# Sums of squares of two chunks, moved on ScalarE from the first feed-forward stage into the opening stage of a delta-rule kernel

## The chip, the core and the metric

The kernel runs on one core of one Trainium2 chip. Five engines of the core work side by side, each through its own list of instructions, strictly in order: TensorE (PE, matrix products and transposes, with its weight loads shown apart as PEld), VectorE (DVE), ScalarE (ACT), GpSimd (POOL) and SyncE (SP, which here only issues transfers). An engine whose next instruction waits for another engine does nothing until that wait is over, even if later instructions of its list could run. The metric is the time of one execution on the device in microseconds (us). Seven runs of the kernel before have a median of 671.46 us, from 670.96 to 672.62.

## What is computed

The first half is a delta-rule attention over 768 tokens, 4 batches and 8 heads of width 48. Keys are divided by their norm, and each head keeps a 48x48 state:

```python
k_n = k / (np.linalg.norm(k, axis=-1, keepdims=True) + 1e-06)
for t in range(S):
    kt, vt, bt = (k_n[:, :, t], v[:, :, t], beta[:, :, t, None])
    y[:, :, t] = np.einsum('bhd,bhde->bhe', q[:, :, t], state)
    v_old = np.einsum('bhde,bhd->bhe', state, kt)
    state = state + bt[:, :, :, None] * np.einsum('bhd,bhe->bhde', kt, vt - v_old)
```

The second half is a feed-forward layer over the 3072 token rows of width 384: `h = x @ w_in` (2048 columns), exact Gelu, and `@ w_out` back to 384 columns. The weights arrive as 64-bit floats.

## The kernel before

Tokens are cut into twelve chunks of 64. A unit is one chunk of two batches, so a chunk has two units (`u.a` is 0 or 1), and a unit's keys are a tile of 128 partitions (2 batches x 64 tokens) by 8 heads by 48. Chunks are worked in pairs, called groups: group 0 is chunks 0 and 1, group 1 is chunks 2 and 3. Within a chunk the recurrence becomes a triangular system. Its diagonal 32x32 blocks are inverted on VectorE by 30 row steps (`eliminate`, L442 and L444, two instructions each), the blocks are joined by small matmuls (`join`, L484, L495, L499), and the result, `Zf`, is multiplied with the right-hand sides (`solve`, L597, copied from PSUM by ScalarE at L603). Then come the outputs (`use`, `read`, L615, L636), their transposes (`turn`, L659, L660), the state update (L624, L629) and the feed-forward layer of the chunk (`fc1` L677 with its Gelu L679 on ScalarE, `fc2` L690).

The kernel has two parts.

The first part, from `load_v(0)` at L827 to L911, is the opening stage. In it the order on all five engines is the order in which the instructions stand in the program (`manual_schedule` over all of them). It loads the keys and queries of chunks 0 and 1, squares and sums their keys, makes their Gram products, starts the row steps of group 0 on VectorE, and while these run lets TensorE and ScalarE make the transposed queries of chunks 0 and 1 (`transposed(u, (1,))`), the score products (`queries`) and the transposes and Gram products of chunks 2 (`third`) and 3 (`fourth`). Each of these is a step of TensorE into PSUM followed by a copy on ScalarE: `Qt` and `Kt` at L347, `P` at L399, `G` at L378, `diag` at L382 and L385. PSUM results of the transposes share two buffers (tag `sq`), products share two others (tag `dn`), so TensorE can be at most two results ahead of ScalarE's copies. The keys of chunk 3 lie in `Qp[2]` and `Qp[3]` in this stage and are loaded again into `Kp` later. After the row steps come the joins, `Zf` (L457 on VectorE, the zeroing L464 and copies L499 on ScalarE), the solve of chunk 0, its outputs, and the decoding of the first pieces of the 64-bit weights. Decoding piece n takes four VectorE steps and one of ScalarE: `begin` (L218), `exponents` (L223, on ScalarE), `mantissas` (L228, L230), `signed` (L235, L236); `signed` needs the result of `exponents`. After `signed`, SyncE fetches another raw piece into the space just freed (L210).

The second part is a plan: every step has a due time in units of chunks (`at(first, last, steps)`), and all steps are written out in the order of their due times (L810). On VectorE that written order is kept. On the other engines a planner orders the instructions by that sequence and by when its own cost model believes their inputs to be ready. The decode of pieces 3 to 15 is in the plan between 0.985 and 1.65. The 32 sums of squares for chunks 2 and 3, `sum_of_squares(u, h)`, one per unit and head, are due between 1.08 and 1.5: an ACTIVATE with the function Square on 128x48 elements at L291, with the sum over the 48 taken from ScalarE's accumulator, which shows in the profile as a second instruction, ACTIVATION_READ_ACCUMULATOR. Their results lie in one tile, `ns["both"]`; its square root is taken on GpSimd at 1.51 (`prep`, L306), and the factors of group 1 are made from it on VectorE at 1.65 (`finish_both`, L265 to L269).

Of the kernel before, what the change touches and what calls it, by code (L numbers as in the profile page):

```python
# [8 lines left out]
F32 = mybir.dt.float32  # L9
# [3 lines left out]
ACT = mybir.ActivationFunctionType  # L13
# [3 lines left out]
def kernel(  # L17
# [28 lines left out]
    nc = tc.nc  # L46
    B, H, S, D = q.shape
# [5 lines left out]
    NA = B // 2  # L53
# [9 lines left out]
    wk = ctx.enter_context(tc.tile_pool(name="wk", bufs=2))  # L63
# [8 lines left out]
    def sq(name, *shape):  # L72
        return small[0].tile([128, *shape], F32, tag="sq", name=name)
# [4 lines left out]
    Qp = [cpool.tile([128, H, C], F32, name=f"Qp{i}") for i in range(NQS)]  # L78
# [12 lines left out]
    tiles = {}  # L91
# [7 lines left out]
    for c in range(NC):  # L99
        for a in range(NA):  # L100
            u = tiles[c, a] = Unit()
# [37 lines left out]
    def load_v(c):  # L139
        if c >= NC:  # L140
            return
        for a in range(NA):
            u = tiles[c, a]
            u.V = io.tile([128, H, D], F32, tag="V", name="V", bufs=4)
            fetch_in(u.V, v, u)
# [111 lines left out]
    def heads(ap):  # L257
        return ap.rearrange("q (j r) d -> q r j d", r=2)
# [24 lines left out]
    def sum_of_squares(u, h):  # L283

        if "both" not in ns:
            n23 = wk.tile([128, 2 * NA, H], F32, tag="n0", name="n0", bufs=1)
            ns[2], ns[3] = n23[:, 0:NA], n23[:, NA:]
            ns["both"] = n23
        if h == 0:
            u.ksq = wk.tile([128, H, D], F32, tag="ksq", name="ksq")  # L290
        nc.scalar.activation(u.ksq[:, h], u.Kn[:, h, 0:D], ACT.Square,  # L291
                             accum_out=ns[u.c][:, u.a, h:h + 1])

    def prep(c):
# [40 lines left out]
    def transposed(u, part=(0, 1)):  # L335
        for x in part:
            if x == 0:
                dst = u.Kt = wk.tile([128, 2, NP, C], F32, tag="Kt", name="Kt", bufs=6)
            elif u.c == 1:
                dst = u.Qt = su.tile([128, 2, NP, C], F32, tag="Qt1", name="Qt1")  # L340
            else:
                dst = u.Qt = wk.tile([128, 2, NP, C], F32, tag="Qt", name="Qt")
            psT = sq("psT", NP, 128)
            flat = (Qp[2 + u.a] if u.c == 3 and x == 0 else (u.Kp, u.Qp)[x]).rearrange("q h d -> q (h d)")
            for j in range(NP):
                nc.tensor.transpose(psT[:, j, :], flat[:, j * 128:(j + 1) * 128], ident)  # L346
            nc.scalar.copy(dst.rearrange("q p j n -> q j p n"),  # L347
                           psT.rearrange("q j (p n) -> q j p n", p=2))
# [11 lines left out]
    def products(us, x):  # L360

        psG = dn("psG").rearrange("q r (m n) -> q r m n", n=C)
        for i, u in enumerate(us):
            for j in range(NP):
                for r, p in QUADS:
                    rows = slice(r * C, r * C + D)
                    nc.tensor.matmul(psG[HALF[p], r, i * NP + j, :], lhsT=u.Kt[rows, p, j, :],  # L367
                                     rhs=(u.Qt if x else u.Kt)[rows, p, j, :],
                                     start=True, stop=True)
        return psG[:, :, 0:len(us) * NP]  # L370

    def grams(us):
        g = us[0].c // 2
        psG = products(us, 0)
        if us[0].t == 0:
            Gs[g] = (wk if g else su).tile([128, NU, HB], F32, tag="G", name="G", bufs=1)
        span = slice(us[0].t * H, (us[-1].t + 1) * H)
        nc.scalar.copy(heads(Gs[g][:, span]), psG[:, :, :, HB:C])  # L378
        if g > 0:
            if us[0].t == 0:  # L380
                Ds[g] = wk.tile([128, NU, HB], F32, tag="diag", name="diag", bufs=1)
            nc.scalar.copy(heads(Ds[g][:, span]), psG[:, :, :, 0:HB])  # L382
            for p in range(2):
                lower = slice(p * C + HB, (p + 1) * C)
                nc.scalar.copy(Ds[g][lower, span], Gs[g][lower, span])  # L385
# [3 lines left out]
    def queries(us):  # L389
        c = us[0].c  # L390
        psP = products(us, 1)
        if c not in Ps:
            Ps[c] = (su if c == 1 else wk).tile([128, NA * H, C], F32, tag=f"P{c == 1}", name="P",
                                                bufs=1)
        for u in us:
            u.P = Ps[c][:, u.a * H:(u.a + 1) * H]
        dst = heads(Ps[c][:, us[0].a * H:(us[-1].a + 1) * H])
        if c < 2:
            nc.scalar.copy(dst, psP)  # L399
        else:  # L400
            both = mask.unsqueeze(1).to_broadcast([128, len(us) * H, C])
            nc.vector.tensor_tensor(dst, psP, heads(both), op=ALU.mult)  # L402
# [259 lines left out]
    def state_steps(c):  # L662
        us = [tiles[c, a] for a in range(NA)]
        steps = [(3.0, against_state, us), (2.0, solve, us), (3.0, outputs, us)]
        return steps + [(0.5, turn, u) for u in us]
# [126 lines left out]
    def ffn_steps(c):  # L792
        ones = [(1.3, fc1, c, f) for f in range(NF)]
        if c > 1:
            return [(1.3, first_layer, c, f) for f in range(NF)] + [
                (2.6, second_layer, c, n) for n in (1, 5, 2, 6, 4, 7, 3)]
        twos = [(2.7, fc2, tiles[c, a], f, f + 4) for a in range(NA) for f in range(0, NF, 4)]
        if c == 0:
            twos.sort(key=lambda s: s[3])
        return ones + twos  # L800

    def at(first, last, steps):

        total, done, timed = sum(s[0] for s in steps), 0.0, []
        for w, *step in steps:
            timed.append((first + (last - first) * (done + 0.5 * w) / total, step))
            done += w
        return timed
# [5 lines left out]
    def signs(c0, c1):  # L814
        psB = sq("psB", c1 - c0, B * H)
        for c in range(c0, c1):
            nc.tensor.transpose(psB[:, c - c0, :], bt[:, c].rearrange("n p t -> n (p t)"),
                                ident[0:B * H, 0:B * H])
        for p in range(2):
            src = psB[HALF[p]].rearrange("q c (a p h) -> q c a p h", p=2, h=H)[:, :, :, p, :]  # L820
            nc.scalar.mul(beta_m[HALF[p], c0:c1], src, -1.0)
# [10 lines left out]
    n0 = wk.tile([128, 2 * NA, H], F32, tag="n0", name="n0", bufs=1)  # L832
# [16 lines left out]
    for u in first:  # L849
        grams([u])  # L850
    signs(2, NC)
    for u in first:
        transposed(u, (1,))
        queries([u])
    for a in range(NA):
        fetch_in(tiles[2, a].Qp[:, :, 0:D], q, tiles[2, a])
# [4 lines left out]
    for n in range(n_in, n_in + len(slots)):  # L861
        fetch(n)
    load_v(1)
    third = [tiles[2, a] for a in range(NA)]
    for u in third:
        transposed(u, (0,))
    grams(third)
    for u in third:
        transposed(u, (1,))
    fourth = [tiles[3, a] for a in range(NA)]  # L870
    for u in fourth:
        transposed(u, (0,))
    grams(fourth)
    for fn, *args in rows:
        fn(*args)
    nc.vector.scalar_tensor_tensor(ng, gms[0][:, 0:NA], -1.0, ns[0], ALU.mult, ALU.mult)
# [40 lines left out]
    def late():  # L917
# [3 lines left out]
        for a in range(NA):  # L921
# [3 lines left out]
            for c in range(5, NC, 2):  # L925
                tiles[c, a].Kb = Kb

    plan = [at(c + 1, c + 2, ffn_steps(c)) for c in range(NC)]
    plan += [at(0.985, 1.26, decode_steps(3, n_in)), at(1.26, 1.65, decode_steps(n_in, NW)), at(1.66, 1.67, [(1.0, late)])]
    plan += [at(0.98, 0.985, [(1.0, load, 3)]),  # L930
             at(1.02, 1.1, [(1.0, join, 0, range(NA, 2 * NA), level) for level in range(2)]),
]
    sums = [(1.0, sum_of_squares, tiles[c, a], h) for c in (2, 3) for a in range(NA) for h in range(H)]
    plan += [at(1.08, 1.5, sums), at(1.51, 1.511, [(1.0, prep, c) for c in (2, 3)]), at(1.65, 1.655, [(1.0, finish_both)]), at(2.97, 2.971, [(1.0, finish, 4)]), at(2.675, 2.676, [(1.0, queries, third)]),
             at(1.12, 1.6, state_steps(1)),
             at(1.75, 2.45, eliminate_steps(1)),
             at(2.58, 2.74, join_steps(1)), at(2.72, 2.98, state_steps(2)),
# [75 lines left out]
```

## Time and profile before

| what | value |
|---|---|
| median of 7 runs | 671.46 us (670.96 to 672.62) |
| the profiled execution | 671.46 us, of which 669.7 us span from first to last instruction |
| PE busy | 642.4 us, 96% of the span |
| DVE busy | 452.0 us, 67% |
| ACT busy | 229.3 us, 34% |
| POOL busy | 81.8 us, 12% |
| mean granted TensorE clock | 0.985 |
| sums of squares of chunks 2 and 3 (L291) | 32 pairs of ACT instructions, first at 59.5 us, last at 75.9 us |

All times in the profile count from the start of the span. A line of the timeline gives the start, the time from there to the end (several like instructions merged as `xN`), the engine, the line of the program, the operation with its output and input, and, in brackets, how long the engine sat idle before it and what ended that wait. The ends of two neighbouring instructions of one engine may overlap by about 0.1 us, since the next one begins while the last one drains. The page cuts the span into 40 slices of 16.7 us; a digit is the busy share in tenths.

### The profile page before, as it was taken

The page shows a single profiled execution, that of the slowest core. Times are in us where ns is not written, and L with a number is a line of the kernel's source. Part 1 is how long each engine was busy: PE and PEld are TensorE (multiplying, and loading weights), DVE is VectorE, ACT ScalarE, POOL GpSimd, SP SyncE. Part 2 cuts the span into 40 slices and gives each one's busy share as a digit, 9 for nine tenths or more (in the row PEclk, how much of TensorE's full clock was granted, in tenths as well). Part 3 has the DMA queues.
Part 4 walks back from the last instruction along what each step waited for, and adds up shares of the span by engine and source line. Part 5 has one row for each costly group of instructions (what it writes and reads, how often), then busy time and mean ns, then how long its engine had stood idle before and what let it go on. Part 6 is the DMA issues. An engine that isn't in the chain of part 4 may idle for free.

```text
span 669.7 us, 21705 instructions
## 1 busy us (share of the span) xinstructions
PE 642.4 (96%) x9542; PEld 560.4 (84%) x9542; DVE 452.0 (67%) x921; ACT 229.3 (34%) x605; POOL 81.8 (12%) x82
## 2 busy tenths in 40 slices
PE   6768999999999999999999999999999999999997
PEld 5656775876789989989989989989989989989997
DVE  6999999994699846489846479846479844324021
ACT  3367754714342143142143142143142133122220
POOL 4051300104011021111021111021111010000000
PEclk9976999999999999999999999999999999999999
DMA  9786555203432232511242511211301310100101
GB/s 132 165 261 172 115 170 139 47 1 68 81 50 36 51 53 41 82 32 32 54 60 37 84 28 26 53 21 32 67 3 24 55 19 3 24 2 2 24 1 25
DMA packets 158431, 39.76 MB, mean 59 GB/s; under 512 B 150016, under 2 KB 153216, under 8 KB 158336
## 3 DMA queue, kind: packets, MB, share of 16 engines
q1 hardware_dynamic: 152464, 33.40, 26.6%
q10 hardware_dynamic: 5872, 4.97, 3.2%
q8 instruction: 75, 1.23, 0.8%
q14 instruction: 20, 0.16, 0.1%
HBM read 33.62 MB, written 4.72 MB: 57 GB/s over the span
## 4 chain that ended last, share of the span: by engine, by line
PE 87%; DVE 6%; ACT 3%; issue 2%; DMA 1%; SPq 0%; ACTq 0%
PE psH L677 36%; PE psX L715 12%; PE psY L715 12%; PE psG L367 5%; PE psZ L715 4%; PE psO L690 4%; PE psK L572 3%; PE psJ L517 3%; PE psU L597 2%; PE psT L346 2%; PE psY L615 2%; DVE w_e L235 1%; PE psY L624 1%; DVE w_out_sb L236 1%; PE psX L659 1%
## 5 line engine op out<-in xcount | busy, mean ns | idle before, releaser
L677 PE MATMUL psH<-xT,w_in_sb 128*128 128x256 f32 x1152 | 262.5, 384 | 1.7 <-ACT G L679 1.5
L677 PEld LDWEIGHTS psH<-xT,w_in_sb 128*128 128x128 f32 x1152 | 215.9, 191 | 33.4 <-ACT G L679 3.4
L679 ACT ACTIVATE G<-psH 128x256 f32<-128x256 f32 x192 | 73.5, 383 | 179.7 <-PE psH L677 167.6
L444 DVE TENSOR_TENSOR Nu<-Nu,tmp 128x30 f32<-128x30 f32 (+9 forms) x180 | 63.9, 355 | 6.2
L442 DVE TENSOR_TENSOR tmp<-Nu 128x30 f32<-128x30 f32 (+9 forms) x180 | 59.3, 330 | 5.1
L715 PE MATMUL psX<-w_out_sb,G 128*128 128x192 f32 x320 | 56.2, 329 | 0.0
L715 PE MATMUL psY<-w_out_sb,G 128*128 128x192 f32 x304 | 54.2, 329 | 0.6
L715 PEld LDWEIGHTS psX<-w_out_sb,G 128*128 128x128 f32 x320 | 52.2, 190 | 0.7
L715 PEld LDWEIGHTS psY<-w_out_sb,G 128*128 128x128 f32 x304 | 49.1, 190 | 2.1 <-DVE u L761 1.8
L690 PE MATMUL psO<-w_out_sb,G 128*128 128x384 f32 x128 | 45.4, 496 | 1.6 <-DVE w_out_sb L236 1.6
L660 ACT COPY xT<-psX 128x384 f32<-128x384 f32 x24 | 11.4, 479 | 103.6 <-PE psX L659 101.7
L306 POOL TENSOR_TENSOR n<-n,half 128x16 f32<-128x16 f32 x10 | 29.4, 2938 | 87.0 <-DVE n L281 66.0
L690 PEld LDWEIGHTS psO<-w_out_sb,G 128*128 128x128 f32 x128 | 23.0, 190 | 17.3 <-DVE w_out_sb L236 4.0
L603 ACT COPY U<-psU 64x192 f32<-64x192 f32 x96 | 30.1, 314 | 20.3 <-PE psU L597 19.1
L402 DVE TENSOR_TENSOR P<-psG,mask 128x1024 f32<-128x1024 f32 x10 | 12.2, 1224 | 35.3 <-PE psG L367 35.3
L466 POOL MEMSET Zf<- 32x512 f32 x23 | 12.4, 540 | 153.9 <-DVE Zf L457 153.0
L580 DVE TENSOR_TENSOR W<-psK,V 128x384 f32<-128x384 f32 x22 | 12.2, 553 | 28.2 <-ACT y L579 28.1
L724 DVE TENSOR_TENSOR S<-G 128x512 f32<-128x512 f32 x20 | 13.7, 687 | 25.8 <-ACT G L679 25.7
L332 POOL TENSOR_TENSOR V<-V,n 128x384 f32<-128x384 f32 x18 | 16.9, 942 | 108.1 <-DMA V<-in_v_dram 81.6
L638 DVE TENSOR_TENSOR x<-psY,y 64x192 f32<-64x192 f32 x80 | 28.2, 353 | 0.9
L715 PE MATMUL psY<-T,G 128*128 128x192 f32 x160 | 28.2, 329 | 0.0
L715 PE MATMUL psX<-T,G 128*128 128x192 f32 x160 | 28.1, 329 | 0.0
(138 smaller groups left out, 869.0 us busy)
## 6 DMA issues: line engine op xcount, KB each, us to landing
Kp<-in_k_dram SPq DMA_DIRECT2D x76, 96.0 KB, 3.6
w_out_sb<-in_moe_w_in_dram SPq DMA_DIRECT2D x24, 256.0 KB, 4.1
V<-in_v_dram SPq DMA_DIRECT2D x48, 96.0 KB, 3.1
out_dram<-o_sb ACTq DMA_DIRECT2D x46, 96.0 KB, 2.2
w_raw<-in_moe_w_out_dram SPq DMA_DIRECT2D x10, 384.0 KB, 3.7
Zf<-in_moe_w_out_dram SPq DMA_DIRECT2D x6, 384.0 KB, 5.1
Qp<-in_q_dram SPq DMA_DIRECT2D x64, 32.0 KB, 2.3
Qp<-in_q_dram SPq DMA_DIRECT2D x16, 96.0 KB, 4.4
```

Source lines behind the costliest of these rows:

```text
L306: nc.gpsimd.tensor_tensor(flat, flat, half, op=ALU.pow)
L367: nc.tensor.matmul(psG[HALF[p], r, i * NP + j, :], lhsT=u.Kt[rows, p, j, :], rhs=(u.Qt if x else u.Kt)[rows, p, j, :], start=True, stop=True)
L442: nc.vector.tensor_tensor(tmp, nu[:, j + 1:, j:j + 1].to_broadcast([128, n, j]), nu[:, j:j + 1, 0:j].to_broadcast([128, n, j]), op=ALU.mult)
L444: nc.vector.tensor_tensor(nu[:, j + 1:, 0:j], nu[:, j + 1:, 0:j], tmp, op=ALU.add)
L517: nc.tensor.matmul(psJ[to, i, :], lhsT=(xm if level else off)[rows, u, :], rhs=zf[rows, u, HB:C] if level else xm[rows, u, :], start=True, ...
L572: nc.tensor.matmul(u.psK[to, x, r, j, :], lhsT=(u.Qt if x else u.Kt)[rows, p, j, :], rhs=St[rows, u.a, p, j, :], start=True, stop=True)
L603: copy(pairs(u.U[HALF[p]], s), u.psU[HALF[p ^ s], p])
L638: nc.vector.tensor_tensor(dst, src, pairs(u.y[HALF[p ^ s]], s), op=ALU.add)
L677: nc.tensor.matmul(psH, lhsT=w_in_sb[:, f // 2, m, f % 2 * 128:(f % 2 + 1) * 128], rhs=xTs[c][:, m, :], start=(m == 0), stop=(m == NM - 1))
L679: nc.scalar.activation(G[:, f, :], psH, ACT.Gelu)
L690: nc.tensor.matmul(u.psO, lhsT=G[:, f, u.a * 128:(u.a + 1) * 128], rhs=w_out_sb[:, f, :], start=(f == 0), stop=(f == NF - 1))
L715: nc.tensor.matmul(ps_, lhsT=lhs[:, f, :], rhs=rhs[:, f, :], start=first and f == 0, stop=f == FH - 1, skip_group_check=not first)
```

## The change

All 32 sums of squares leave the plan and go into the opening stage, still on ScalarE:

- Four of chunk 2 stand between the `Qt` copy and the `queries` of each of the units 2 and 3 of `first` (the two units of chunk 1), eight in all, all on unit 0 of chunk 2.
- The other eight of chunk 2 stand after the `Kt` transposes of `third` and ahead of its Gram products.
- All sixteen of chunk 3 stand after the Gram products of `fourth` and ahead of what follows the row steps.

Since the keys of chunk 3 lie in `Qp[2 + a]` at that time, `sum_of_squares` reads them there. The tile of the results takes its space from the tag `root` instead of `n0`, because the `n0` tile of chunks 0 and 1 is still in use then.

```diff
     def sum_of_squares(u, h):
 
         if "both" not in ns:
-            n23 = wk.tile([128, 2 * NA, H], F32, tag="n0", name="n0", bufs=1)
+            n23 = wk.tile([128, 2 * NA, H], F32, tag="root", name="n23", bufs=1)
             ns[2], ns[3] = n23[:, 0:NA], n23[:, NA:]
             ns["both"] = n23
         if h == 0:
             u.ksq = wk.tile([128, H, D], F32, tag="ksq", name="ksq")
-        nc.scalar.activation(u.ksq[:, h], u.Kn[:, h, 0:D], ACT.Square,
+        kn = Qp[2 + u.a] if u.c == 3 else u.Kn
+        nc.scalar.activation(u.ksq[:, h], kn[:, h, 0:D], ACT.Square,
                              accum_out=ns[u.c][:, u.a, h:h + 1])
...
     signs(2, NC)
+    third = [tiles[2, a] for a in range(NA)]
+    some = iter([(u, h) for u in third for h in range(H)])
     for u in first:
         transposed(u, (1,))
+        for i in range(4 if u.t > 1 else 0):
+            sum_of_squares(*next(some))
         queries([u])
...
-    third = [tiles[2, a] for a in range(NA)]
     for u in third:
         transposed(u, (0,))
+    for left in some:
+        sum_of_squares(*left)
     grams(third)
     for u in third:
         transposed(u, (1,))
...
     for u in fourth:
         transposed(u, (0,))
     grams(fourth)
+    for u in fourth:
+        for h in range(H):
+            sum_of_squares(u, h)
     for fn, *args in rows:
         fn(*args)
...
-    sums = [(1.0, sum_of_squares, tiles[c, a], h) for c in (2, 3) for a in range(NA) for h in range(H)]
-    plan += [at(1.08, 1.5, sums), at(1.51, 1.511, [(1.0, prep, c) for c in (2, 3)]), at(1.65, 1.655, [(1.0, finish_both)]), ...
+    plan += [at(1.51, 1.511, [(1.0, prep, c) for c in (2, 3)]), at(1.65, 1.655, [(1.0, finish_both)]), ...
```

More of the change, by code (lines that the diff above doesn't have):

```diff
@@ L932 @@
 ]
-    sums = [(1.0, sum_of_squares, tiles[c, a], h) for c in (2, 3) for a in range(NA) for h in range(H)]
-    plan += [at(1.08, 1.5, sums), at(1.51, 1.511, [(1.0, prep, c) for c in (2, 3)]), at(1.65, 1.655, [(1.0, finish_both)]), at(2.97, 2.971, [(1.0, finish, 4)]), at(2.675, 2.676, [(1.0, queries, third)]),
+    plan += [at(1.51, 1.511, [(1.0, prep, c) for c in (2, 3)]), at(1.65, 1.655, [(1.0, finish_both)]), at(2.97, 2.971, [(1.0, finish, 4)]), at(2.675, 2.676, [(1.0, queries, third)]),
              at(1.12, 1.6, state_steps(1)),
```

## The prediction

> **What bounds the kernel now.** I read the page first, for what binds which stretch.
>
> ```profile
> span 669.7 us, 21705 instructions
> ...
> PE 642.4 (96%) x9542; PEld 560.4 (84%) x9542; DVE 452.0 (67%) x921; ACT 229.3 (34%) x605; POOL 81.8 (12%) x82
> ...
> DVE  6999999994699846489846479846479844324021
> ACT  3367754714342143142143142143142133122220
> ```
>
> Slices are 16.7 us. In slices 2 to 9 DVE is at 90% or more; the same page has PE at 60 to 80% in slices 1 to 4 and at 90% or more from there. ACT is dense only in slices 3 to 5 (33 to 84 us), in the last two of which the squares lie. So the question is whether ACT in that stretch holds anybody up, and what ACT holds up in the stretch to which the squares go. The timeline of ACT answers the second half.
>
> ```profile
> 29.60 0.59 ACT L399 COPY P<-psG 128x512 f32<-128x512 f32 x1 [1.25 <-PE psG L367]
> ...
> 34.32 0.59 ACT L347 COPY Kt<-psT 128x512 f32<-128x512 f32 x1 [0.27 <-PE psT L346]
> 36.10 0.59 ACT L378 COPY G<-psG 128x512 f32<-128x512 f32 x1 [1.19 <-PE psG L367]
> ...
> 44.02 1.24 ACT L385 COPY diag<-G 32x512 f32<-32x512 f32 x2
> 47.70 0.63 ACT L464 ACTIVATE Zf<-low 32x512 f32<-32x512 f32 x1 [2.44 <-DVE Zf L457]
> ...
> 49.87 0.94 ACT L223 ACTIVATE w_e<-w_e,lim 128x768 uint32<-128x768 uint32 x1
> ...
> 53.86 0.94 ACT L223 ACTIVATE w_e<-w_e,lim 128x768 uint32<-128x768 uint32 x1
> ...
> 58.66 0.94 ACT L223 ACTIVATE w_e<-w_e,lim 128x768 uint32<-128x768 uint32 x1
> ```
>
> At 29.60 and 36.10 ACT sat idle 1.25 and 1.19 us for PE: gaps. At 47.70 it waited 2.44 us for DVE's second half of `Zf`: the last gap. From there ACT works through zeroing, copies, decode and outputs to 58.66 in one go, with no wait over 0.5 us. The pieces of that run are each other's cause: PE waits for these copies, and ACT for PE's short answers.
>
> ```profile
> 43.77 0.86 DVE L495 TENSOR_TENSOR XM<-psJ,gm 32x256 f32<-32x256 f32 x2
> 44.78 0.86 DVE L495 TENSOR_TENSOR XM<-psJ,gm 32x256 f32<-32x256 f32 x2 [0.15 <-PE psJ L484]
> 45.67 1.93 DVE L457 STREAM_TRANSPOSE Zf<-Nu 128x1024 f32<-128x1024 f32 x1
> ...
> 59.63 0.96 DVE L235 SCALAR_TENSOR_TENSOR w_e<-w_out_sb,w_e 128x768 uint32<-128x768 uint32 x1 [0.92 <-ACT w_e L223]
> ...
> 88.40 0.96 DVE L235 SCALAR_TENSOR_TENSOR w_e<-Zf,w_e 128x768 uint32<-128x768 uint32 x1 [0.41 <-ACT w_e L223]
> ```
>
> The timeline of DVE shows who depends on that run. At 44.78 DVE has no slack against PE's joins (0.15 us idle). At 59.63 `signed(2)` waits 0.92 us for ACT's exponents, the instruction at 58.66. From 59.63 to the end of the weight decode, 117.29, DVE is back to back; its one wait above 0.2 us is the 0.41 at 88.40.
>
> ```profile
> 39.11 1.97 PE L346 MATMUL psT<-ident,Qp 128*128 128x128 f32 x8 [2.06 <-ACT Qt L347]
> ...
> 44.04 0.69 PE L484 MATMUL psJ<-XM,G 32*32 32x32 f32 x32 [0.58 <-ACT diag L382]
> ...
> 117.43 2.85 PE L690 MATMUL psO<-w_out_sb,G 128*128 128x384 f32 x8 [0.48 <-DVE w_out_sb L236]
> ```
>
> The timeline of PE gives both ends. At 39.11 the transposes of chunk 3 waited 2.06 us for ACT's `Qt` copy to free a PSUM buffer; at 44.04 the second join waited for ACT's `diag` copy. At 117.43 PE waits for the last decoded weight piece; after it PE is all but full, and its later waits, such as 1.28 us between 150 and 160 for the next joins, follow DVE's row steps, which start where the decode ends. So the path that sets the end runs through ACT until 59, through DVE's decode until 117, then through PE. A delay of ACT at 47.7 is a delay of the end unless the decode gives it back; a saving of ACT at 60 to 76 is a saving only as far as it shortens DVE's decode.
>
> **The frame.** The profiled execution took 671.46 us, 669.7 of span and 1.76 around it; that is also the median of the seven runs, so changes are added to 671.46 directly.
>
> **The price of a sum of squares.** The rows of L291:
>
> ```profile
> L291 ACT ACTIVATE ksq<-Kp x32: 225/232/238, 59.5 to 75.9; 128x48 f32<-128x48 f32 x32
> L291 ACT ACTIVATION_READ_ACCUMULATOR ksq<-Kp x32: 185/191/197, 59.6 to 76.0; 128x1 f32 x32
> L291 ACTq EVENT_SEMAPHORE  x4: 17/38/38, 58.3 to 71.1; - x4
> ```
>
> The two overlap. In an unbroken row of them, from 66.19 to 67.32 us, five pairs take 1.13 us: 0.226 us a pair. 32 pairs are 7.2 us of ACT. ScalarE: Activation LUTs, section "What ACT_TABLE_LOAD costs", gives an ACTIVATE with immediates 186 ns plus 0.833 ns an element, and 93 ns of overlap between neighbours; by that, as an estimate, a square would follow another every 0.133 us. The trace agrees for the first of the pair (0.13 us from its start to the start of the read) but the page has no line for the read of the accumulator, which adds 0.09. By the page's price all groups of squares would fit their gaps and the sum would be -0.3 us. The measured pitch decides; the sum below uses it alone.
>
> **Edits that cost nothing, and their cover.** The new place of the result tile must wait for the last reader of the root's scratch tile, done on DVE at 12.5 us; the first square comes at 28.3. The scratch of the squares has two buffers, last read at 9.7. Keys of chunk 2 are issued by SP from 18.77 to 20.8 and land 5.3 to 5.8 us later, by 26.6: 1.7 us to spare. Keys of chunk 3 are issued from 27.76 on and land in 2.9 us, ten microseconds before they are squared. No DMA moves in any queue. SP's later load of queries into the space of chunk 3's keys must now also wait for the squares, but stands at 63.3 us. GpSimd's two roots, at 68.5 and 76.3, waited 16.4 and 4.6 us for the squares; they come earlier, and their reader is DVE at 117.29, so nothing follows.
>
> **The first eight squares.** Four stand behind the `Qt` copy that ends at 28.35, and the next instruction, the `P` copy, starts at 29.60. 4 x 0.226 = 0.90 fits into the 1.25. The same at 31.21 to 32.45. Cost 0; the cover left is 0.35 us, and beyond that each microsecond of squares would be one of delay.
>
> **The next eight.** They follow the `Kt` copy that starts at 34.32. A 512-wide copy lets the next instruction begin after 0.48 us (36.10 to 36.58), so they begin at 34.80 and end for the queue at 34.80 + 8 x 0.226 = 36.61. The `G` copy behind them started at 36.10: **+0.51**. Queued behind it are `diag`, its two patches and the `Qt` copies; PE's transposes of chunk 3 wait for those (39.11), ACT's copies of their Gram product for PE, PE's second join for ACT (44.04) and DVE for that join at 44.78. No slack anywhere, so DVE's `Zf` at 45.67 also goes later by 0.5, to 46.2. Between 0.4 and 0.65, for where a copy lets a square begin.
>
> **The sixteen of chunk 3.** The last patch copy lets go of ACT at 45.16 (44.02 plus 1.24, less 0.1 of overlap), now 45.67. 16 x 0.226 = 3.62 takes ACT to 49.29. The zeroing of `Zf` behind them, ready in 48.2 on DVE's side, started at 47.70: **+1.59**, in which the 0.51 is contained. Queued behind it: four `Zf` copies for which PE's solve waits, both exponents, sixteen copies of `U` and `x`, two of `xT`. DVE had waited 0.92 us for the exponents of piece 2 already, so its `signed(2)` moves from 59.63 by the full 1.59. Bounds 1.3 and 2.0: the one if the queue lets go 0.3 earlier, the other if chunk 3's copies start late by one PSUM round (0.43, the idle time ahead of the `Kt` copies).
>
> **What the removal gives back.** 7.2 us of ACT leave 59.5 to 76, but DVE shows waits there for ACT of 0.41 at 88.40 alone, plus 0.16 at 77.59 beyond its usual pitch. The 0.41 comes from exponents behind eight `U` copies, which came late with PE; PE had waited 0.71 us at 66.34 for a Gelu behind squares. If PE gains that, the 0.41 goes. The give-back lies between 0 and 0.57; I take 0.3, nearer to the wait that has a cause in the squares. That PE waits less for Gelus is worth nothing in itself: what it gains, it waits at 110 to 117 for decoded weights (0.17, 0.94 and 0.48 us).
>
> PE's clock was granted at 0.50 from 47 to 63 us by the windows, so a longer pause ahead of the solve finds PE slow already and makes it no slower; the pause is costed at nothing.
>
> **Sum.** +1.59 - 0.3 = +1.3 us: 672.8 us, or +0.19%. About 0.2%, 1.34 us, is what a measurement of this kernel can tell from no change, so my forecast is slower, at the edge of what can be told.
>
> **Rivals.**
>
> 1. Not slower: PE's three waits for decoded weights, 0.17 + 0.94 + 0.48 = 1.59 us, get filled. With ACT free the planner may see chunk 1's transposed outputs sooner and put some of its feed-forward matmuls ahead of the last `psO`. Then 672.8 - 1.6 = 671.2. It decides from 1.3 us of such work on. For it: PE is ahead by up to 0.71 us after 66. Against: `psH` and `psO` share two PSUM buffers, and both hold `psO` until the copy at 119.02.
> 2. The planner's new order costs. With the squares gone it may put Gelus or `U` copies ahead of exponents; eight `U` copies last 2.6 us, one exponent 0.94. One such turn in the decode, where DVE has no slack, adds 0.9 to 2.6: 673.7 to 675.4, say 674.0. For it: the wait at 88.40 is of this kind. Against: exponents had mostly been waiting for DVE, as by 1.72 us at 92.32.
> 3. The change does not cost what I say: all squares hide in the gaps. At 0.159 us a pair or less the eight end by 36.10 (1.30 us of room) and the sixteen by 47.70 (2.54 us), cost 0, less 0.3: 671.2. Against: all 32 pairs of before kept at or above 0.22.
>
> **How the numbers follow.** My forecast 0.54, its own range 672.2 to 673.5 (1.3 - 0.57 and 2.0 - 0), half of it on each side of 672.8. Rival 1 0.18, two fifths of it under 670.1 if the planner gains more than the waits; rival 2 0.20; rival 3 0.08, a third of it with a further planner's gain. Slower by over 0.2%: 0.27 + 0.20 = 0.47. Faster: 0.07 + 0.03 = 0.10. Same: the rest, 0.43. The range reaches from 671.0, just under rival 1, to 674.0, rival 2's value, which leaves out some 0.1 on each side.
>
> **What would show it.** Right: ACT's `G` copy of chunk 2 near 36.6, the zeroing of `Zf` near 49.3 with no wait for DVE ahead of it, the U copies near 52.8, `signed(2)` on DVE near 61.2, the end of the decode near 118.6, and PE's span after it unchanged at 552 us (117.4 to 669.7). Wrong: the zeroing still waiting for DVE, a decode that ends before 118, or PE with other work between its last `psO` groups. What would make the prediction wrong most easily is the planner: the order on ACT and PE after 59 us is not the program's, and I read from before only that it had little to gain.

## The result

The changed kernel takes 673.13 us in the median of 14 runs (672.25 to 674.89), against 671.43 of the kernel before in 35 runs beside it (670.1 to 673.08). The ratio is 1.0029, with a 95% interval of 1.0022 to 1.0036: slower by 1.9 us, 1.5 to 2.4, where the medians alone differ by 1.7. The profiled execution took 672.25 us, with a span of 670.5; it is the fastest of the 14, so what it shows of the cost may be less than the average. Line numbers below are those of the changed kernel, one higher than before for most of what follows L291. Every experiment has its own numbers, again one or a few higher.

Its page, with span, busy times and the slices of DVE and ACT:

```profile
span 670.5 us, 21710 instructions
...
PE 640.9 (96%) x9542; PEld 559.0 (83%) x9542; DVE 452.5 (67%) x921; ACT 229.5 (34%) x605; POOL 83.2 (12%) x82
...
DVE  6999989995699846479846479846479844324021
ACT  3496444714342143142143142143142133122220
```

ACT is heavier in the second and third slice (4 and 9 tenths for 3 and 6 before) and lighter in the fourth to sixth (6, 4 and 4 for 7, 7 and 5): the work moved as described. PE's and DVE's busy times stayed within 1.5 us. The lines of ACT that answer to those shown of before, from its timeline:

```profile
27.50 0.59 ACT L348 COPY Qt<-psT 128x512 f32<-128x512 f32 x1 [0.43 <-PE psT L347]
...
29.34 0.59 ACT L400 COPY P<-psG 128x512 f32<-128x512 f32 x1 [0.35 <-PE psG L368]
...
36.37 0.56 ACT L379 COPY G<-psG 128x512 f32<-128x512 f32 x1
...
43.04 1.24 ACT L386 COPY diag<-G 32x512 f32<-32x512 f32 x2
...
48.03 0.63 ACT L465 ACTIVATE Zf<-low 32x512 f32<-32x512 f32 x1
...
83.94 2.59 ACT L604 COPY U<-psU 64x192 f32<-64x192 f32 x8 [1.55 <-PE psU L598]
86.56 0.66 ACT L680 ACTIVATE G<-psH 128x256 f32<-128x256 f32 x2
88.59 0.38 ACT L680 ACTIVATE G<-psH 128x256 f32<-128x256 f32 x1 [1.38 <-PE psH L678]
88.87 0.93 ACT L223 ACTIVATE w_e<-w_e,lim 128x768 uint32<-128x768 uint32 x1
```

`Qt` at 27.50 is followed by four squares (left out), and ACT still waits 0.35 us before the `P` copy. Ahead of the `G` copy at 36.37 there is no wait any more, nor ahead of the zeroing of `Zf` at 48.03: both gaps are used up. But the zeroing is only 0.33 us later than before, 47.70. The four lines from 83.94 on are a second difference, far from the squares: behind the `U` copies stand three Gelus, the third waits 1.38 us for PE, and the exponents of weight piece 8 come last, at 88.87. In the kernel before, these exponents stood behind two Gelus, with no wait:

```profile
84.27 2.59 ACT L603 COPY U<-psU 64x192 f32<-64x192 f32 x8 [0.72 <-PE psU L597]
86.88 0.66 ACT L679 ACTIVATE G<-psH 128x256 f32<-128x256 f32 x2
87.43 0.94 ACT L223 ACTIVATE w_e<-w_e,lim 128x768 uint32<-128x768 uint32 x1
```

VectorE and TensorE of the changed kernel:

```profile
41.94 1.93 DVE L458 STREAM_TRANSPOSE Zf<-Nu 128x1024 f32<-128x1024 f32 x1
...
45.66 1.95 DVE L458 STREAM_TRANSPOSE Zf<-Nu 128x1024 f32<-128x1024 f32 x1
...
60.03 0.96 DVE L235 SCALAR_TENSOR_TENSOR w_e<-w_out_sb,w_e 128x768 uint32<-128x768 uint32 x1 [0.92 <-ACT w_e L223]
...
89.83 0.96 DVE L235 SCALAR_TENSOR_TENSOR w_e<-Zf,w_e 128x768 uint32<-128x768 uint32 x1 [1.62 <-ACT w_e L223]
```

```profile
39.35 1.15 PE L347 MATMUL psT<-ident,Qp 128*128 128x128 f32 x8 [2.91 <-ACT Qt L348]
...
118.87 2.85 PE L691 MATMUL psO<-w_out_sb,G 128*128 128x384 f32 x8 [0.48 <-DVE w_out_sb L236]
```

On DVE, `signed(2)` at 60.03 still waits 0.92 us; `signed(8)` at 89.83 waits 1.62 us for those exponents, where it waited 0.41. At PE, the transposes of chunk 3 at 39.35 took 1.15 us for 1.97 before: PE's clock was full there. The last decoded weights arrive at 118.87, 1.44 us later than before.

The row steps do not begin at the same time in every profile: their first transpose of `Nu` starts between 13.91 and 15.33 us, over all kernels. So the table counts from R, the start of DVE's first transpose of `Zf` after the row steps (41.94 in the DVE lines above, 41.80 before). Each entry is the start of an instruction in the profile, less R, in us; only the wait of `signed(8)` is DVE's idle time ahead of it. The clock is what the windows of 39 to 41, 41 to 43 and 43 to 45 us show for PE (1.00 is full, 0.50 is half).

| kernel | clock, three windows | zeroing of `Zf` | `signed(2)` | wait of `signed(8)` | end of decode |
|---|---|---|---|---|---|
| before | 0.53, 0.62, 1.00 | 5.90 | 17.83 | 0.41 | 75.49 |
| changed | 1.00, 1.00, 0.97 | 6.09 | 18.09 | 1.62 | 76.79 |
| changed, again | 1.00, 1.00, 0.83 | 5.86 | 17.83 | 1.10 | 77.12 |
| chunk 3 only | 1.00, 1.00, 0.67 | 6.15 | 18.11 | 1.68 | 76.87 |
| squares added | 0.50, 0.50, 0.50 | 7.20 | 19.12 | 1.54 | 77.82 |
| changed, exponents first | 0.71, 0.50, 0.50 | 6.96 | 18.88 | none | 76.01 |
| chunk 2 only | 1.00, 1.00, 1.00 | 5.74 | 17.71 | 0.62 | 75.42 |
| no squares | 0.68, 0.50, 0.50 | 5.79 | 17.71 | 0.34 | 75.45 |
| before, exponents first | 1.00, 1.00, 0.89 | 5.75 | 17.67 | none | 74.84 |
| both exponents early | 1.00, 1.00, 0.56 | 5.76 | 16.70 | none | 74.28 |
| the same, 20 squares in gaps | 1.00, 1.00, 1.00 | 5.76 | 16.81 | none | 74.26 |

The end of the decode is read as the start of `finish_both` on DVE (L265), which follows the last `signed` at once: 117.29 before and 118.73 in the changed kernel. The other kernels are those of the next section.

### The profile page after: what moved, and what is told of

It reads as the page before. It is cut to its first block, busy times and chain, and to the rows that moved or that the text cites. A ratio compares the mean times of both kernels' runs of the same rounds, so it can differ in the third digit from the quotient of the medians.

```text
span 670.5 us, 21710 instructions
## 1 busy us (share of the span) xinstructions
PE 640.9 (96%) x9542; PEld 559.0 (83%) x9542; DVE 452.5 (67%) x921; ACT 229.5 (34%) x605; POOL 83.2 (12%) x82
## 4 chain that ended last, share of the span: by engine, by line
PE 85%; DVE 10%; issue 2%; ACT 2%; DMA 1%; SPq 0%; DVEq 0%; ACTq 0%
PE psH L678 37%; PE psX L716 12%; PE psY L716 12%; PE psZ L716 4%; PE psO L691 4%; PE psK L573 3%; PE psJ L518 3%; PE psG L368 3%; PE psU L598 2%; PE psY L616 2%; DVE tmp L443 2%; DVE Nu L445 2%; DVE w_e L235 1%; PE psY L625 1%; DVE w_out_sb L236 1%
## 5 line engine op out<-in xcount | busy, mean ns | idle before, releaser
L445 DVE TENSOR_TENSOR Nu<-Nu,tmp 128x30 f32<-128x30 f32 (+9 forms) x180 | 62.0, 344 | 6.2
L443 DVE TENSOR_TENSOR tmp<-Nu 128x30 f32<-128x30 f32 (+9 forms) x180 | 61.0, 339 | 5.1
```

The costliest lines, as they stand in the source:

```text
L443: nc.vector.tensor_tensor(tmp, nu[:, j + 1:, j:j + 1].to_broadcast([128, n, j]), nu[:, j:j + 1, 0:j].to_broadcast([128, n, j]), op=ALU.mult)
L445: nc.vector.tensor_tensor(nu[:, j + 1:, 0:j], nu[:, j + 1:, 0:j], tmp, op=ALU.add)
```

## The experiments

My theory after the result: two separate costs. The squares of chunk 3 hold up ACT's zeroing of `Zf` by an amount that depends on PE's clock, and they make the planner set exponents 8 late. The rivals: the removal from the plan disturbs the planner; or the prediction's sum, in which the whole 1.6 us come from the opening stage.

### Squares added in the opening, none removed

```diff
+    def squared_again(u, h):     # as sum_of_squares, into a scratch tile
...
         transposed(u, (1,))
+        for i in range(4 if u.t > 1 else 0):
+            squared_again(*next(some))
...
     grams(fourth)
+    for u in fourth:
+        for h in range(H):
+            squared_again(u, h)
```

> The squares of the change are added to the opening stage, at the places of the change, into a scratch tile that nobody reads; the plan keeps its own 32 as before. So 7.2 us of ScalarE work are added and none is taken away. Theory: the opening costs, by two ways. It holds ScalarE by up to 1.6 us before the zeroing of Zf (0.33 us in the one profile of the changed kernel, where TensorE's clock was full at 39 to 43 us), and it makes the planner believe that ScalarE comes later, so that the planner sets the exponents of weight piece 8 behind eight U copies and three Gelus, as in the changed kernel; VectorE then waits 1.2 us longer there. Sum +1.5 to +2.8 us, 673.0 to 674.3. Rival: what costs is that the squares are gone from the plan, which changes the planner's order; then this kernel costs the opening's delay alone, +0.3 to +1.6, and the wait at exponents 8 stays near 0.4 us.

Measured: 673.7 us, ratio 1.0036 (1.0024 to 1.0048), or +2.4 us. Zeroing and `signed(8)`, from the timelines of ACT and DVE:

```profile
48.87 0.63 ACT L474 ACTIVATE Zf<-low 32x512 f32<-32x512 f32 x1
```

```profile
90.59 0.96 DVE L235 SCALAR_TENSOR_TENSOR w_e<-Zf,w_e 128x768 uint32<-128x768 uint32 x1 [1.54 <-ACT w_e L223]
```

The zeroing is at 48.87, 7.20 us after R and 1.3 later than before, and the wait of 1.54 us at 90.59 is there although no square left the plan. The rival, that the removal is to blame, falls.

### No squares at all

```diff
+    n23 = wk.tile([128, 2 * NA, H], F32, tag="root", name="n23", bufs=1)
+    nc.gpsimd.memset(n23, 0.5)
...
-        for i in range(4 if u.t > 1 else 0):
-            sum_of_squares(*next(some))
...
-    for u in fourth:
-        for h in range(H):
-            sum_of_squares(u, h)
```

> The 32 sums of squares of chunks 2 and 3 are left out altogether: their tile is filled with 0.5 by GpSimd in the opening stage. The opening's ScalarE list is that of before, the plan's is without the squares. Theory: removing the squares from the plan costs nothing; it gives back at most VectorE's wait of 0.41 us for exponents 8 and 0.16 at 77.6: -0.6 to 0.0 us, 670.9 to 671.4. The end of the decode, 117.29 us before, comes at 116.7 to 117.3. Rival: the removal disturbs the planner's order, and VectorE's wait for exponents 8 grows to 1.6 us as in the changed kernel: +1.2 us, 672.6.

The diff is against the changed kernel; a constant stands where the sums would be. Measured: 670.94 us, ratio 0.9997 (0.9988 to 1.0006). Taking 7.2 us of ACT work away altogether is worth at most 0.8 us and perhaps nothing. The wait at exponents 8 is 0.34 us: the order of before. So the squares were hardly a burden in the plan, and as long as the order of the rest stays, no place for them could have gained more than that.

### The changed kernel, exponents of piece 8 first

```diff
-        nc.scalar.activation(G[:, f, :], psH, ACT.Gelu)
+        with tc.issue_after(exps[n_in]) if c == 0 and f > 10 else ExitStack():
+            nc.scalar.activation(G[:, f, :], psH, ACT.Gelu)
```

`exps[n]` holds the instruction of `exponents(n)`; `issue_after` orders what follows on the same engine behind it.

> The changed kernel, with one more rule for the planner: the Gelus of chunk 0 from the twelfth on stand behind the exponents of weight piece 8 on ScalarE. The squares are where the change puts them. Theory: VectorE's wait of 1.62 us at 89.8 us falls to 0 to 0.2 and the end of the decode comes 1.4 to 1.6 us earlier than in the changed kernel; against the kernel before only the opening's delay is left, less what the wait of 0.41 was worth: -0.2 to +1.2 us, 671.3 to 672.6. Rival: the wait is not on the path, since the Gelus that now go later hold TensorE instead: the time stays at +1.7 us, 673.1.

Measured: 671.45 us, ratio 1.0003 (0.9995 to 1.0012). The wait is gone from DVE's timeline, and by the ratios about 1.7 us of the change's 1.9 are gone with it; 0.41 us of that wait stood in the kernel before too, so the next run puts the same rule there. TensorE had cover for the later Gelus, so that rival falls. The zeroing lies at 6.96 in this profile, with PE's clock at 0.71 and then 0.50.

### The kernel before, exponents of piece 8 first

> The kernel before, with the same rule: the Gelus of chunk 0 from the twelfth on stand behind the exponents of weight piece 8. Theory: VectorE's decode is the path, so the wait of 0.41 us at 88.4 goes and the end comes 0.4 to 0.5 us earlier: 670.9 to 671.1. Rival: TensorE, which loses 0.9 us of cover to the Gelus, becomes the path there: 671.5 to 672.3.

The edit is the same. Measured: 670.5 us, ratio 0.9993 (0.9985 to 1.0002), so about 0.5 us less, not clear of zero. With the same order on both sides, what is left between this and the run before is the opening stage: 1.0003 against 0.9993, about 0.7 us on average, with intervals that overlap a little.

### Chunk 2 alone, and chunk 3 alone

```diff
-    sums = [... for c in (2, 3) for a in range(NA) for h in range(H)]
+    sums = [... for c in (2, 3) for a in range(NA) for h in range(H) if c == 3]
```

The squares of chunk 2 move as in the change, those of chunk 3 stay; in the other run the reverse, with `if c == 2`.

> Only the sixteen squares of chunk 2 move, to the places of the change; those of chunk 3 stay in the plan as before. Theory: the sixteen of chunk 3 are what costs. Here the eight ahead of the Gram products of chunk 2 delay ScalarE by 0.5 us, which ends in the 2.4 to 4.0 us for which ScalarE waits for VectorE before it zeroes Zf; only where TensorE is cold at 39 to 45 us does VectorE's second join lose up to 0.5. The planner's order at weight piece 8 stays that of before, so VectorE's wait there is 0.1 to 0.4 us: -0.3 to +0.4 us in all, 670.9 to 671.6. Rival, that of the prediction's sum: the half-microsecond goes on in full, and it is 671.5 to 671.9.

> Only the sixteen squares of chunk 3 move, to the place of the change; those of chunk 2 stay in the plan as before. Theory: this is where nearly all of the change's cost is. 3.6 us of squares in a gap of 2.4 us when TensorE is cold, of 4.0 when it is not: 0 to 1.2 us; and the planner, which then believes ScalarE later, sets exponents 8 behind three Gelus, with a wait of 1.5 us on VectorE instead of 0.4: +1.1. Sum +1.1 to +2.3, 672.3 to 673.4. Rival: the cost comes from both groups alike; then half of it, +0.9, 672.0.

Measured: chunk 2 alone 671.71 us, ratio 1.0005 (0.9996 to 1.0014); chunk 3 alone 672.7 us, ratio 1.0021 (1.0012 to 1.0030). The zeroing and the exponents' wait in chunk 2 alone and then in chunk 3 alone, from the timelines of ACT and DVE:

```profile
48.46 0.63 ACT L465 ACTIVATE Zf<-low 32x512 f32<-32x512 f32 x1 [3.61 <-DVE Zf L458]
```

```profile
89.25 0.96 DVE L235 SCALAR_TENSOR_TENSOR w_e<-Zf,w_e 128x768 uint32<-128x768 uint32 x1 [0.62 <-ACT w_e L223]
```

```profile
47.72 0.63 ACT L465 ACTIVATE Zf<-low 32x512 f32<-32x512 f32 x1
```

```profile
89.55 0.96 DVE L235 SCALAR_TENSOR_TENSOR w_e<-Zf,w_e 128x768 uint32<-128x768 uint32 x1 [1.68 <-ACT w_e L223]
```

With chunk 2 alone ACT's `G` copy of chunk 2 also came without a wait, yet ACT stood idle for 3.61 us before the zeroing: the half microsecond ends there. PE's clock was full in this profile; what becomes of the half microsecond at half clock it does not show. With chunk 3 alone there is no wait left before the zeroing, and exponents 8 are late by 1.68. So the late exponents follow the sixteen squares ahead of `Zf`, wherever the rest of the squares are. That the planner does so because its model then has ACT, and with it the start of chunk 0's feed-forward layer, later is my reading of it; the runs show only which squares bring it about.

### Exponents of piece 2 earlier

```diff
-    for u in first[:NA]:
-        turn(u)
+    turn(first[0])
+    begin(2)
+    exponents(2)
+    turn(first[1])
     for u in first[:NA]:
         update(u)
-    begin(2)
-    exponents(2)
     mantissas(2)
```

This is the kernel before, with that and with the exponents of piece 8 first.

> The kernel before, with the exponents of weight piece 8 ahead of the Gelus as in the earlier run, and the exponents of weight piece 2 in the opening stage moved ahead of the second transposed output of chunk 0. No square moves. Theory: VectorE's decode from 59.6 to 117.3 us is the path, and it begins with a wait of 0.92 us for these exponents; the wait goes, the decode starts 0.9 us earlier, and TensorE, whose first feed-forward matmuls start 0.4 us later, has cover for it: -0.9 on top of the -0.5 of the rule for piece 8, 669.9 to 670.3. Rival: TensorE's late start or the arrival of raw weights takes the place of the wait: 670.6 to 671.3.

Measured: 669.75 us, ratio 0.9977 (0.9967 to 0.9987): 1.5 us faster than the kernel before, clear of it and of the changed kernel. DVE's timeline at the start of the decode and where a new wait appears:

```profile
58.28 0.96 DVE L236 SCALAR_TENSOR_TENSOR w_e<-w_out_sb,w_e 128x768 uint32<-128x768 uint32 x1
...
76.66 0.56 DVE L218 TENSOR_SCALAR w_e<-w_out_sb 128x768 uint32<-128x768 uint32 x1 [0.49 <-DMA Qp<-in_k_dram]
```

`signed(2)` at 58.28 follows its predecessor without a wait. Of the 1.0 us gained there against the run with piece 8 alone (16.70 for 17.67 after R), 0.6 arrive at the end of the decode (74.28 for 74.84): at 76.66 DVE now waits 0.49 us for a transfer. Some 1.4 us less were expected; 1.5 were measured, with an interval of 0.9 to 2.2. The rival, that raw weights arrive too late, holds for the 0.4 us lost on the way. The path is what the prediction took it for: ACT until 59 us, DVE's decode until 117.

### Twenty squares in the gaps

```diff
     for u in third:
         transposed(u, (0,))
+    for i in range(4):
+        sum_of_squares(*next(some))
...
     grams(fourth)
+    for h in range(H):
+        sum_of_squares(fourth[0], h, True)
```

Eight more stand behind the `Qt` copies as in the change, twelve stay in the plan, and both exponents are early.

> Twenty of the 32 squares move, only as many as the gaps hold: eight of chunk 2 behind the Qt copies, four ahead of the Gram products of chunk 2, eight of chunk 3 behind those of chunk 3; the other twelve stay in the plan. With it both moves of exponents of the run before this one. Theory: squares in gaps cost nothing and give next to nothing, since VectorE's decode holds no wait for them: the same time as without the moved squares, 669.9 to 670.3. Rival: ScalarE's relief after 60 us is worth something once the exponents are out of the way: 669.2 to 669.7. Other rival: squares cost even in the gaps: 670.6 to 671.2.

Measured: 670.28 us, ratio 0.9983 (0.9974 to 0.9992). The same line of ACT's timeline:

```profile
48.19 0.63 ACT L466 ACTIVATE Zf<-low 32x512 f32<-32x512 f32 x1 [1.70 <-DVE Zf L459]
```

ACT still waits 1.70 us there, and the decode ends 74.26 us after R, as without moved squares (74.28). The medians differ by half a microsecond, within their intervals. Squares in gaps cost nothing that can be seen and bring nothing, as far as half a microsecond can be told.

### Keeping TensorE busy in its pause

```diff
+    idle = ps.tile([128, 256], F32, tag="mlp", name="idle")
+    for i in range(9):
+        nc.tensor.matmul(idle, lhsT=ident, rhs=low.rearrange("q a b -> q (a b)")[:, 0:256],
+                         start=i == 0, stop=i == 8)
     fourth = [tiles[3, a] for a in range(NA)]
```

> The changed kernel with the rule for the exponents of weight piece 8, and with nine more matmuls of 128x256 on TensorE, whose result nobody reads, between the transposed queries of chunk 2 and the transposes of chunk 3, where TensorE otherwise stands idle for two to three microseconds. Theory: what the squares of chunk 3 cost in the opening depends on TensorE's clock at 39 to 45 us. In the profiles so far the zeroing of Zf on ScalarE began 6.1 and 6.15 us after the row steps' first Zf transpose where the clock there was mostly full, 6.96 and 7.20 where it was about half, and 5.75 to 5.90 in kernels without those squares, whatever the clock. With TensorE kept busy the clock is full there, the zeroing begins 6.0 to 6.2 us after the transpose, and the end of the decode comes 75.2 to 75.5 us after it, against 76.2 without the extra matmuls; the time is 0.2 to 0.8 us below that of the kernel without them, so 0 to 0.5 us below the kernel before. Rival: the clock follows the squares' length, not the pause, or the extra matmuls hold the transposes up: the zeroing at 6.9 or later, time as before or above.

Measured: 677.54 us, ratio 1.0095 (1.0075 to 1.0115), far outside of what either theory gave. PE's timeline in the opening, and PE's longest wait later on:

```profile
36.03 4.05 PE L880 MATMUL idle<-low,ident 128*128 128x256 f32 x18
39.92 1.04 PE L348 MATMUL psT<-ident,Qp 128*128 128x128 f32 x8
```

```profile
155.43 0.21 PE L519 MATMUL psJ<-XM,G 32*32 32x32 f32 x1 [2.36 <-issue]
155.43 0.26 PE L519 MATMUL psJ<-Zf,XM 32*32 32x32 f32 x1
```

The clock was full from 39 to 43 us, as meant. But the nine matmuls show as eighteen instructions and 4.05 us, and held the transposes until 39.92, some half a microsecond too long; the zeroing came 6.49 us after R. That is better than the 6.96 and 7.20 at half clock and worse than 6.1; it lies in neither of the ranges expected. The end of the decode, 75.96 after R, is no better than without (76.01), so the loss lies later. There, PE once waited 2.36 us for nothing that the profile shows. By the windows its clock was then 0.50 from 155 to 165 us and 0.69 from 165 to 175, where the run without the nine matmuls has 1.00. PE was busy for 9.57 and 10.00 us of these; as an estimate from these figures that is 7.9 us of work at full clock lost, of the 8.8 us by which the part behind the decode is longer (560.7 for 551.9). But this profile is of the slowest of the six executions, 680.4 us. Three others took 675.81 to 677.12 with a mean clock of 0.985, as high as that of the kernel before in its profile. What costs these about 5 us is open.

That filling the pause brings about a full clock is not shown either: seven of the eleven profiles without the filler have a full clock from 39 to 43 us as well.

### The changed kernel once more

> The changed kernel once more, for one more profile of its opening stage. Theory: the clock at 39 to 45 us is either full or half; if half, the zeroing of Zf begins 6.9 to 7.2 us after the row steps' first Zf transpose instead of 6.1, and VectorE's wait for exponents 8 stays at 1.5 to 1.7 us. If the clock is full, 6.1 again. Rival: the zeroing lies anywhere between, without regard to the clock.

Measured: 672.49 us in its one run. The clock was full, the zeroing came 5.86 us after R, and the wait at exponents 8 was 1.10 us; two waits for weight transfers, 0.41 and 0.51 us at 77.67 and 100.69, take DVE to the same end of the decode and a little beyond. With it there are five profiles with all sixteen squares of chunk 3 ahead of `Zf`, without the filler matmuls: three with a clock at or near full and the zeroing at 5.86 to 6.15, two with about half and 6.96 and 7.20. PE in two of them, from the windows (PEclk is the third number from the end), first the changed kernel, then the run with squares added:

```profile
39.00:41.00 2.00, 1.47 (x28) 1.16 (x32) 1.90 (x7) 1.74 (x4) 1.02 (x2) 1.00 1.00 379
41.00:43.00 2.00, 1.56 (x92) 1.34 (x80) 2.00 (x2) 1.19 (x3) 2.00 (x3) 1.00 1.02 407
```

```profile
39.00:41.00 2.00, 2.00 (x19) 1.67 (x21) 1.93 (x6) 1.02 (x3) 1.29 (x2) 0.50 1.01 393
41.00:43.00 2.00, 2.00 (x78) 1.88 (x75) 2.00 (x2) 0.64 (x2) 2.00 (x3) 0.50 1.03 410
```

The kernels without those sixteen have 5.74 to 5.90 at either clock.

How the clock comes in can be followed through the twelve profiles. From PE's transposes of chunk 3 to ACT's last patch copies of chunk 3 (39.35 to 43.04 in the lines of the changed kernel, 39.11 to 44.02 before) pass 3.63 to 3.70 us in the eight profiles with a full clock from 39 to 43 us, and 4.40 to 5.06 in the four with less, with or without squares. Where the sixteen squares follow, the zeroing starts 4.99 to 5.00 us after these copies do, in all six profiles, the one with the filler included. So the slower chain is what makes the zeroing later; when the clock falls, and why, the runs do not show.

## Why the prediction was right, and where it was not

It said 672.8 us, +1.3, slower at the edge of what can be told; it is 673.13 and +1.9. The direction and the size held. The sum behind them did not: two of its terms were off, in opposite directions, and that they cancelled is luck. Its signs show it. The `G` copy (36.37 for 36.6), the end of the decode (118.73 for 118.6) and the span behind it (551.8 for 552) came as said. On the way the zeroing was at 48.03 for 49.3, the `U` copies at 51.60 for 52.8 and `signed(2)` at 60.03 for 61.2: about 1.2 us early, which the longer wait of `signed(8)` took back.

**The price of a square** was right: 0.226 us a pair in the new place too (44.53 to 47.69 us holds fourteen pairs in 3.16). The measured pitch decided. By the Trainium skill, ScalarE: Activation LUTs, section "What ACT_TABLE_LOAD costs", the estimate is 0.133 us a square; the sixteen would then have ended near 46.4, and ACT would still have waited for DVE. The trace does not agree with that estimate where the accumulator is read as well.

**The edits costed at nothing** show no cost: every group of squares starts right behind the copy ahead of it. **The first eight squares** cost nothing either: the prediction left a cover of 0.35 us, and the profile shows 0.35 at 29.34.

**The next eight** moved the `G` copy by 0.53 us against the `Kt` copy ahead of it (36.37 - 34.06 for 36.10 - 34.32); 0.51 was said. What failed is the next sentence, "no slack anywhere". The slack that the profile of before showed to be nil was nil because PE ran at half clock at 39 to 43 us in that execution. Where the clock is full, as in the changed kernel's profile, the chain through chunk 3 is 1.2 us shorter (3.69 us for 4.91), DVE's joins do not wait, and the second `Zf` starts 3.72 us after R, not later than the 3.87 of before. Chunk 2 alone measured +0.3 us with an interval that holds zero.

**The sixteen of chunk 3** were put at +1.59, which took that one execution's clock for the rule. The profiles give 0 to 0.4 where the clock is full and 1.1 to 1.5 where it is not, and the two runs with the same exponents' order some 0.7 us on average. Mechanism and place were right, the size was more than double.

**The give-back** was put at 0.3 us, between 0 and 0.57. It was a further cost of about 1.2: the wait of `signed(8)` went from 0.41 to 1.62. This is the price of rival 2, which the prediction gave one chance in five: exponents behind `U` copies and Gelus in the decode, at 0.9 to 2.6 us. Its stated cause, the squares gone from the plan, was wrong: without any squares in it the planner kept the order of before, and with all of them left in it and the opening lengthened it did not. What the prediction did not think of is that work added to a stage written out by hand can change the planner's order of what follows; that it does so through the planner's modelled time is not shown.

**Rival 1**, PE's waits for decoded weights filled with other work, did not happen: PE's last three `psO` groups still wait, 0.76, 0.95 and 0.48 us. **Rival 3**, all in the gaps, was out with the pitch, though with a full clock it was nearly so (0 to 0.4 us).

**The frame of the whole**, that ACT until 59 and DVE until 117 set the end and that a relief of ACT after 60 is worth next to nothing, held: no squares at all -0.2 us, two moved exponents -1.5.

## What to carry to other kernels

An idle gap in one profile is a gap of that execution: before filling it, ask what sets its two ends, and whether the engine that sets them ran at full clock just then. Under a planner, read where the instructions that others wait for stand in each engine's list after the change, even far from the edit: here a wait grew by 1.2 us, 40 us later, and one ordering rule took it away. And look first at what the path's engine waits for; two instructions moved on that path brought more than 32 moved beside it.

## What was not expected of the hardware

PE's granted clock after its pause of one to three microseconds near 37 to 39 us was about half in some executions and full in others, without an evident relation to the length of the pause that the transposes of chunk 3 show: from 39 to 43 us it was 1.00 after 1.19 us, 0.53 and 0.62 after 2.06 in one profile and 1.00 after 2.06 in another, 0.50 after 2.81, and 1.00 after 2.92. By windows of one microsecond and less, the clock falls to 0.50 in every one of the twelve profiles, somewhere between 37.7 and 46.0 us, and is full again for good only between 60 and 65. (In the profile of before it was full once more from 42.5 to 45.9.) So what differs is the moment of the fall. In the run with the nine more matmuls it came at 44.9 us, though PE had had no pause over 0.8 us since 35. An early fall costs the kernel before nothing, since the gap ahead of `Zf` takes it up; in the changed kernel that gap is gone.

The other surprise is the run with nine more matmuls at 36 us: its span from the end of the decode on was 560.7 us, where the other profiles have 551.6 to 552.5, with a stall of 2.36 us on PE that no semaphore explains and a clock of 0.50 and 0.69 in the 20 us behind it. Such stalls of up to 1.7 us stand in the profile of before too.
